# Unread products planned by the scheduler, weight loads that wait for earlier ones, and key copies on another engine, in a fused attention and two-layer expert kernel

## The chip, the core and the metric

The kernel runs on one core of a Trainium2 chip. The core has a matrix engine (TensorE, PE in the rows; PEld is its weight load), a vector engine (VectorE, DVE), a scalar engine (ScalarE, ACT), a general engine (GpSimd, POOL) and a queue engine (SyncE, SP) that issues transfers to 16 DMA engines. Each engine works off its own list of instructions in order; a list waits where an instruction needs another engine's result. The metric is the device time of one execution in microseconds (us).

## The reference

Chunked attention with a few memory rows, then two feed-forward layers over 3072 tokens (4 batches of 768), width 512, inner width 2048:

```python
for c in range(nc):                      # chunks of 32 tokens
    k_full = concat(mem_k, k[c_start - 16 : c_end + 8])
    a = softmax(q_c @ k_full.T / sqrt(64))
    out[c] = a @ concat(mem_v, v[...])
h = x @ w_in;  g = h * clip(h + 3, 0, 6) / 6;  x = g @ w_out      # first layer
h = x @ w_in;  g = max(0.01 * h, h);           out = g @ w_out    # second layer
```

Inputs are float32; the weights come as 64-bit floats.

## The kernel before

Matrices are multiplied in a high and a low part (`xh` and `xl`, and the two halves of a tile `w`), three products for each. A weight tile is loaded as 128x1024 words (`decode`, `load`), decoded to 32 bits by one ACT instruction and four on DVE (tiles `wm`, `ys` or `st`), and split in two parts (`split_w`).

The attention is cut into units of 384 tokens and four heads (`unit`) and, near the beginning, half units (`half_unit`). Each goes through the same steps: load queries and keys (`load_qk`), copy the keys' windows next to each other (`windows`), load the value rows (`load_v`, `load_whole`), copy the memory rows into them (`memory`, on POOL), scores on PE, maximum on DVE, exponential on ACT, sum and normalisation on DVE (`norm`), transposes on PE, their copy to SBUF by ACT (`take_p`), value products on PE, and `to_x`, which makes `xh` on ACT and `xl` on DVE. Four of these pieces make the first 512 tokens: two units whose PSUM tiles are `at` and `ab`, and two half units in `h` and `ac`. The products of the first layer (`hidden`, line 1003; `output`, line 1052) begin with these 512 tokens. All later attention lies between such products.

Only keys and a few load places (LOADS, WEIGHTS) are written by hand. Each step is a `Task` with a cost per engine, a key and what it comes after; `schedule` plays the engines through with those costs, picks for each free engine the ready task of the lowest key, and emits its instruction. The order in which instructions stand on each engine follows from that, and changes wherever a cost or constant changes. `feed` models the stream of PE's instructions: so many are held (HELD), and blocks of 256 come after a while (FETCH).

PE also computes products that nobody reads: `warm` multiplies `ident` by itself into the second half of the tile `ac`. They are tasks that come after named steps (`marks`); before `ac`'s scores they are 512 columns wide, behind them 256, and there they go into the tile that holds those scores (`home`). A product of float32 operands appears as two matmuls in the trace.

## Time and profile before

| what | value |
|---|---|
| median of 3 runs (1046.39 to 1047.87) | 1046.4 us |
| the profiled execution | 1049.14 us |
| its span in the profile | 1047.4 us |
| PE busy | 1035.1 us (99%) |
| DVE busy | 875.3 us (84%) |
| ACT busy | 693.7 us (66%) |
| POOL busy | 20.8 us (2%) |
| moved by DMA | 220.49 MB, 211 GB/s |

The span goes from the first to the last instruction of the profiled execution; the execution's own time has a little more around it. The rows below give starts in us from the span's start. In a row of the order of time, what stands in brackets is how long the engine was idle before it and what ended that. "Granted clock" is PE's: 1.00 is 2.4 GHz, 0.50 is 1.2 GHz.

### The profile page before, as it was taken

To read this page: it belongs to the slowest core of one execution; us is meant where nothing else is said; L and a number is where in the kernel's file an instruction comes from. 1 tells how busy PE (TensorE), PEld (TensorE's weight loads), DVE (VectorE), ACT (ScalarE), POOL (GpSimd) and SP (SyncE) were. 2 spreads that over 40 slices of the span, in tenths; PEclk is the share of its full clock that TensorE was granted. 3 is DMA by queue.
4 is the path that set the end of the run, shared out by engine and by line. 5 is a ranking of instruction groups with operands and counts; after the bars stand their busy time and mean duration, and the time that the engine had idled before them with its cause. 6 is when DMAs were issued, how large, how long until landed. Compare 5 with 4: busy or idle time off the path is not lost.

```text
span 1047.4 us, 20225 instructions
## 1 busy us (share of the span) xinstructions
PE 1035.1 (99%) x7476; PEld 850.3 (81%) x7476; DVE 875.3 (84%) x1485; ACT 693.7 (66%) x1480; POOL 20.8 (2%) x30
## 2 busy tenths in 40 slices
PE   7999999999999999999999999999999999999998
PEld 4778988888788888888888888888888888888886
DVE  6898988778998778799999899999576998566775
ACT  4786876655888555476686576785565874666753
POOL 3010000000000000000000000000000000000000
PEclk8899999999999999999999999999999999999999
DMA  9889787876887979673648778546342454423451
GB/s 265 283 216 331 241 291 230 258 229 221 262 282 239 332 225 290 239 239 123 214 144 268 253 251 280 183 158 221 111 171 81 174 193 156 173 109 96 146 181 61
DMA packets 127314, 220.49 MB, mean 211 GB/s; under 512 B 12528, under 2 KB 76016, under 8 KB 127216
## 3 DMA queue, kind: packets, MB, share of 16 engines
q1 hardware_dynamic: 127216, 219.20, 63.9%
q8 instruction: 59, 0.97, 0.4%
q14 instruction: 39, 0.32, 0.1%
HBM read 156.24 MB, written 62.91 MB: 209 GB/s over the span
## 4 chain that ended last, share of the span: by engine, by line
PE 89%; DVE 4%; DMA 3%; ACT 3%; issue 1%; SPq 0%; DVEq 0%; ACTq 0%
PE y L1327 15%; PE y L1052 13%; PE y L1495 12%; PE h L1327 10%; PE h L1495 8%; PE hx L1495 8%; PE h L1003 7%; PE hx L1327 7%; PE h L1052 2%; PE at L639 2%; DMA w<-in_raw 2%; PE at L549 1%; DVE w L345 1%; PE at L607 1%; PE ac L466 1%
## 5 line engine op out<-in xcount | busy, mean ns | idle before, releaser
L345 DVE TENSOR_TENSOR w<-w 128x512 fp32r<-128x512 f32 (+2 forms) x393 | 322.9, 854 | 25.8 <-ACT w L342 23.9
L342 ACT CAST w<-w 128x512 fp32r<-128x512 f32 (+1 forms) x290 | 223.3, 803 | 13.4 <-PE hx L1495 3.6
L1052 PE MATMUL y<-g,w 128*128 128x512 f32 (+1 forms) x540 | 125.2, 375 | 0.9 <-ACT g L342 0.7
L1327 PE MATMUL y<-w 128*128 128x512 f32 x516 | 124.6, 390 | 0.0
L1327 PEld LDWEIGHTS y<-w 128*128 128x128 f32 x516 | 96.6, 188 | 20.1
L1052 PEld LDWEIGHTS y<-g,w 128*128 128x128 f32 x540 | 94.1, 189 | 19.0 <-ACT g L342 1.2
L342 ACT CAST g<-w 128x512 fp32r<-128x512 f32 x80 | 49.4, 620 | 63.8 <-PE y L1495 23.0
L1495 PE MATMUL y<-w 128*128 128x512 f32 x384 | 90.3, 389 | 0.0
L1495 PEld LDWEIGHTS y<-w 128*128 128x128 f32 x384 | 72.1, 188 | 14.9
L1301 ACT ACTIVATE w<-w 128x512 f32<-128x512 f32 x72 | 45.0, 630 | 40.4 <-DVE w L1372 18.1
L1003 PE MATMUL h<-xh,w 128*128 128x512 f32 (+1 forms) x288 | 66.1, 370 | 0.5 <-DVE w L345 0.5
L345 DVE TENSOR_TENSOR g<-w,g 128x512 fp32r<-128x512 f32 x80 | 54.1, 684 | 14.3 <-ACT g L342 14.2
L1495 PE MATMUL h<-w 128*128 128x512 f32 x264 | 62.1, 389 | 0.0
L1495 PE MATMUL hx<-w 128*128 128x512 f32 x252 | 59.2, 389 | 0.0
L1327 PE MATMUL h<-xl,w 128*128 128x512 f32 x240 | 58.3, 391 | 0.0
L1495 PEld LDWEIGHTS h<-w 128*128 128x128 f32 x264 | 49.6, 188 | 10.3
L1003 PEld LDWEIGHTS h<-xh,w 128*128 128x128 f32 x288 | 49.7, 189 | 9.9 <-DVE w L345 0.9
L1495 PEld LDWEIGHTS hx<-w 128*128 128x128 f32 x252 | 47.3, 188 | 9.8
L1327 PEld LDWEIGHTS h<-xl,w 128*128 128x128 f32 x240 | 44.8, 188 | 9.9 <-DVE xl L345 0.4
L1327 PE MATMUL y<-xh,w 128*128 128x512 f32 x216 | 52.2, 390 | 0.0
L1327 PEld LDWEIGHTS y<-xh,w 128*128 128x128 f32 x216 | 40.5, 188 | 8.4
L1052 PE MATMUL y<-w 128*128 128x512 f32 x180 | 46.6, 391 | 0.0
(244 smaller groups left out, 1852.2 us busy)
## 6 DMA issues: line engine op xcount, KB each, us to landing
w<-kept2i SPq DMA_DIRECT2D x42, 512.0 KB
w<-kept2o SPq DMA_DIRECT2D x42, 512.0 KB
w<-kept1i SPq DMA_DIRECT2D x28, 512.0 KB
a<-in_raw SPq DMA_DIRECT2D x20, 448.0 KB
w<-in_w1i SPq DMA_DIRECT2D x16, 512.0 KB
w<-in_w1o SPq DMA_DIRECT2D x16, 512.0 KB
w<-in_w2i SPq DMA_DIRECT2D x16, 512.0 KB
w<-in_w2o SPq DMA_DIRECT2D x16, 512.0 KB
```

What stands on the lines that cost most here:

```text
L342: nc.scalar.copy(out, in_) if e == "ACT" else engine(e).tensor_copy(out=out, in_=in_)
L345: engine(e).tensor_tensor(out=out, in0=a, in1=b, op=ALU.subtract)
L466: nc.tensor.matmul(x, ident, ident.unsqueeze(1).to_broadcast([128, c, 128]), start=True, stop=True, skip_group_check=True)
L549: nc.tensor.matmul(ps.t[h * CHUNK:(h + 1) * CHUNK, par, i * W:(i + 1) * W], qk[h // 2].t[r, gp, (h % 2) * G + c * CHUNK:(h % 2) * G + (c + ...
L607: nc.tensor.transpose(pt.t[:, i // NC, (i % NC) * 128:(i % NC + 1) * 128], pview()[:, i * 128:(i + 1) * 128], ident)
L639: nc.tensor.matmul(pv.t[(h % 2) * D:(h % 2 + 1) * D, par, (h // 2) * 2 * G + i * CHUNK:(h // 2) * 2 * G + (i + 1) * CHUNK], v[h // 2].t[r, ...
L1003: nc.tensor.matmul(h.t[:, o:o + n], w.t[:, 1 if p == 1 else 0, k * 128:(k + 1) * 128], x[:, k, c0:c0 + n], start=(p == 0 and k == 0 and o ...
L1052: nc.tensor.matmul(bank(banks[d])[:, c0:c0 + n], w.t[:, 1 if p == 1 else 0, d * 128:(d + 1) * 128], g.t[:, 1 if p == 2 else 0, at:at + n], ...
L1301: return add(lambda e: nc.scalar.activation(out=at(), in_=at(), func=AF.Prelu, alpha=0.01), {"ACT": act(N)}, key, after=[after], uses=uses)
L1327: nc.tensor.matmul(bank(to), wt(l, o)[:, kt * 128:(kt + 1) * 128].bitcast(F32R), operand(p, name, 1 if q == 2 else 0, kt).bitcast(F32R), s ...
L1495: nc.tensor.matmul(bank(to[d]), wt(1 if q == 1 else 0, o)[:, d * 128:(d + 1) * 128].bitcast(F32R), g.t[:, 1 if q == 2 else 0], start=(fres ...
```

## The change

Unread products: `warm` and `marks` are gone. `schedule` gets a function `filler` and a list of places (`spots`); when PE has no task before the first product of the first layer, it emits a product of 512 columns into a place that is free (`opens` names a tile that becomes free for it at the end of a task, `closes` takes it out). It keeps a rough record of PE's work (`worked`) and doubles costs where that was low.

Weight loads: the third to sixth load get `hold`. A copy of one element on POOL (`follow`) from the weight tile two loads earlier, once that has landed, into the new tile comes ahead of the load, which thereby waits.

Copies: both copies of the keys' windows of the second unit (`ab`) go from DVE to ACT (`windows(i)`, the costs in `unit`). The memory rows (`memory`) are copied by POOL, as they were.

Constants: the costs for transfers, instruction blocks and DVE beside POOL in `schedule`.

```diff
-RATE_QK, RATE, RATE_V, COLD = 380.0, 220.0, 300.0, 1.1
+RATE_QK, RATE, RATE_V, COLD = 380.0, 220.0, 240.0, 1.1
...
-STARTS, LANDS, SURE = 1900.0, 500.0, 1500.0
-HELD, FETCHED, FETCH, STALL = 447, 256, 5000.0, 250.0
+STARTS, LANDS, SURE, SOONER = 1900.0, 250.0, (0.0, 1500.0), 20000.0
+HELD, FETCHED, ASKS, FETCH, STALL = 447, 256, (256, 356), 2500.0, 250.0
+WINDOW, PHASE, IDLE, WATCHED, BESIDE = 3413.0, 4400.0, 2000.0, 80000.0, 0.4
+FIRST, LATER, FIRST_TILL = (512, 1900.0), (512, 880.0), 2500.0
...
-            if comes is None and used >= held - FETCHED:
-                comes = at + FETCH
+            if comes is None and used >= held - ASKS[at > 45000.0]:
+                comes = max(at, max((y for x, y in queued if x <= at), default=0.0)) + FETCH if at < WATCHED else at + 2.0 * FETCH
...
                 if pick is None:
+                    if e == "PE" and not progress and spots and (begun or now < FIRST_TILL):
+                        cols, took = LATER if begun else FIRST
+                        filler(spots[0], cols)
...
+                        free[e] = end
+                        push(end, "free", None)
                     continue
...
+                    d = pick.opts[e]
+                    if now < WATCHED:
+                        at = int((now - PHASE) // WINDOW)
+                        if now < PHASE or worked.get(at - 1, 0.0) < WINDOW - IDLE:
+                            d *= 2.0
...
+                if e == "DVE" and free["POOL"] > now and pick.key < 100:
+                    d += min(BESIDE * d, free["POOL"] - now)
...
+        if hold:
+            before, landed = hold
+
+            def follow(e):
+                nc.gpsimd.tensor_copy(out=make(t, ([128, 512, 2], U32))[:1, 0, :1].bitcast(F32), in_=before.t[:1, 0, :1].bitcast(F32))
+
+            k = add(follow, {"POOL": 100.0}, early, after=[*after, landed], allocs=[t], uses=[before])
+            k = add(load, {"SP": dma(524288, 380.0)}, early, after=[k], uses=[t])
...
+    def filler(b, cols):
+        t = made(b)
+        nc.tensor.matmul((t[:, 1] if b.tag[0] == "a" else t)[:, N - cols:], ident, ident.unsqueeze(1).to_broadcast([128, cols // 128, 128]) if cols > 128 else ident[:, :cols], start=True, stop=True, skip_group_check=True)
...
-        t = [add(windows(i), ({"DVE": 850.0} if i or quad else {"ACT": 1050.0}) if j == 0 else {"ACT": 1050.0}, key - 30, after=[l1[i]], allocs=[kw[i]], uses=[qk[i]]) for i in range(2)]
+        t = [add(windows(i), ({"DVE": 850.0} if i and not quad else {"ACT": 1050.0}) if j == 0 else {"ACT": 1050.0}, key - 30, after=[l1[i]], allocs=[kw[i]], uses=[qk[i]]) for i in range(2)]
...
-    warm(2)
-    warm(1, marks["s", 0, 0])
-    warm(2, marks["s", 0, 1])
-    warm(1, marks["s", 1, 0, 0])
-    home = marks["b", 1, 1, 0][0]
-    for m, n in ((("s", 1, 1, 0), 2), (("t", 0, 0), 3), (("t", 0, 1), 3), (("t", 1, 1, 0), 2), (("v", 1, 0, 0), 2)):
-        warm(n, marks[m], home)
...
+            parts = decode(src, f, at - 8, early[i] if i < len(early) else min(at - 38, 6 * i - 40), splits[before:before + 1] if before >= 0 else (), "ys" if i % 2 else ("wm", "st")[f // 2 % 2] if alone_ else "wm", gate=behind if 3 <= i < 6 else (), own=alone_, split=which if alone_ else None, hold=arrivals[i - 2] if 2 <= i < 6 else ())
```

What that moves, at three places. PE from the unread product behind the first unit's scores on, before; `ident` as an operand means an unread product where the shape is 512 or 256 wide, and a transpose where it is 128 wide; `64x32` are value products, `32x64` scores:

```order
L466 MATMUL ac<-ident 128x512
L549 MATMUL ab<-w 32x64 x48
L466 MATMUL ac<-ident 128x512 x2
L816 MATMUL h<-w 32x64 x24
L466 MATMUL ac<-ident 128x512
L816 MATMUL ac<-w 32x64 x24
L607 MATMUL at<-ident,w 128x128 x6
L466 MATMUL ac<-ident 128x256 x5
L627 MATMUL at<-w 64x32 x48
L607 MATMUL ab<-ident,w 128x128 x6
L466 MATMUL ac<-ident 128x256 x3
```

and the same stretch after the change:

```order
L505 MATMUL ac<-ident 128x512 x2
L586 MATMUL ab<-w 32x64 x48
L505 MATMUL ac<-ident 128x512 x3
L853 MATMUL h<-w 32x64 x24
L644 MATMUL at<-ident,w 128x128 x6
L505 MATMUL ac<-ident 128x512
L853 MATMUL ac<-w 32x64 x24
L664 MATMUL at<-w 64x32 x48
L644 MATMUL ab<-ident,w 128x128 x6
L908 MATMUL h<-ident,w 128x128 x3
L505 MATMUL h<-ident 128x512
L908 MATMUL ac<-ident,w 128x128 x3
```

The transposes of `at` stand ahead of `ac`'s scores now, no unread product stands between those scores and `at`'s value products, and the two that are left before the first product go into `h`, one on each side of `ac`'s transposes.

DVE between the reciprocal of the first unit's sums and its normalisation (`TENSOR_TENSOR w<-w,mx 128x768`), before; the copies are the windows of the keys of the half unit in `ac`:

```order
L599 RECIPROCAL mx<-mx 128x12
L342 COPY w<-w 128x2x3x56
L342 COPY w<-w 128x2x3x8
L342 COPY w<-w 128x2x3x56
L342 COPY w<-w 128x2x3x8
L603 TENSOR_TENSOR w<-w,mx 128x768
```

and after:

```order
L636 RECIPROCAL mx<-mx 128x12
L640 TENSOR_TENSOR w<-w,mx 128x768
L375 COPY w<-w 128x2x3x56
L375 COPY w<-w 128x2x3x8
L375 COPY w<-w 128x2x3x56
L375 COPY w<-w 128x2x3x8
```

The normalisation now stands ahead of the copies.

SP from the last value rows of the first 512 tokens (`L783`) on, before; the pieces of 56x3x128 and 8x3x128 are value rows of the next half unit, the 128x2x448 in front of them its queries and keys, 128x1024 a weight tile:

```order
L783 DMA w<-in_raw 64x2x128 x2
L394 DMA w<-in_w1i 128x1024
L394 DMA w<-in_w1o 128x1024
L394 DMA w<-in_w1i 128x1024
L394 DMA w<-in_w1o 128x1024
L774 DMA w<-in_raw 128x2x448
L790 DMA w<-in_raw 56x3x128
```

and after:

```order
L820 DMA w<-in_raw 64x2x128 x2
L427 DMA w<-in_w1i 128x1024
L427 DMA w<-in_w1o 128x1024
L811 DMA w<-in_raw 128x2x448
L827 DMA w<-in_raw 56x3x128
```

The fifth and sixth weight load have moved behind the queries and keys of the next half unit and the eight pieces of its value rows.

## Rows read from the trace of the kernel before

**Rows 1.** Busy time by stage: stretch, its length, engines, granted clock, DMA share, GB/s.

```profile
30.00:40.00 10.00, 10.00 (x262) 8.19 (x261) 7.85 (x22) 6.57 (x21) 0.00 (x0) 0.85 0.71 208
40.00:50.00 10.00, 8.83 (x82) 6.56 (x82) 9.85 (x25) 9.92 (x33) 0.00 (x0) 1.00 0.85 308
...
400.00:500.00 100.00, 100.00 (x443) 82.83 (x442) 89.17 (x148) 62.70 (x100) 0.00 (x0) 1.00 0.65 216
```

**Rows 2.** The page's first line.

```profile
span 1047.4 us, 20225 instructions
```

**Rows 3.** PE in order of time: start, duration, line, operation, count.

```profile
1.36 3.78 PE L466 MATMUL ac<-ident 128*128 128x512 f32 x4 [1.36 <-POOL three L308]
...
8.73 1.45 PE L549 MATMUL ab<-w 64*32 64x64 f32 x96
10.11 1.99 PE L466 MATMUL ac<-ident 128*128 128x512 f32 x4
...
14.37 0.45 PE L816 MATMUL h<-w 64*32 64x64 f32 x29 [1.40 <-issue]
...
17.28 1.51 PE L607 MATMUL at<-ident,w 128*128 128x128 f32 x6
...
23.62 2.08 PE L466 MATMUL ac<-ident 128*128 128x256 f32 x4 [1.97 <-ACT w L850]
25.62 2.97 PE L627 MATMUL at<-w 64*64 64x32 f32 x96
...
39.77 2.17 PE L1003 MATMUL h<-xh,w 128*128 128x512 f32 x8
...
47.28 1.20 PE L1052 MATMUL y<-g,w 128*128 128x512 f32 x4 [0.67 <-ACT g L342]
```

**Rows 4.** Waits of PE, 40 to 1040 us: total, times, longest.

```profile
PE y L1052 <- ACT g L342: 0.7, 1, 0.7
PE at L871 <- DVE w L867: 0.5, 1, 0.5
...
PE hx L1327 <- DVE w L1294: 0.2, 1, 0.2
```

**Rows 5.** ACT in order of time, 0 to 20 us.

```profile
4.58 1.11 ACT L342 COPY w<-w 128x336 f32<-128x336 f32 x4 [2.35 <-DMA w<-in_raw]
11.10 0.84 ACT L573 ACTIVATE w<-w 128x768 f32<-128x768 f32 x1 [5.41 <-DVE w L568]
...
18.89 0.80 ACT L342 COPY w<-at 128x768 f32<-128x768 f32 x1
```

**Rows 6.** Busy time and granted clock of three stretches, columns as in rows 1.

```profile
13.00:14.40 1.40, 0.03 (x5) 0.03 (x6) 1.03 (x3) 1.40 (x11) 1.19 (x2) 1.00 1.22 324
16.00:19.50 3.50, 3.46 (x56) 2.72 (x57) 3.43 (x12) 1.32 (x4) 1.21 (x2) 0.50 1.11 312
29.60:33.00 3.40, 3.40 (x12) 2.73 (x11) 2.96 (x7) 0.88 (x2) 0.00 (x0) 0.50 0.84 231
```

**Rows 7.** The chain that ended last: later value products of a whole unit.

```profile
82.32 1.55 PE at L639 x96
```

**Rows 8.** DVE in order of time, 9 to 17 us.

```profile
9.01 0.07 DVE L563 MEMSET at<- 128x16 f32 x1
...
15.51 0.77 DVE L342 COPY w<-w 128x336 f32<-128x336 f32 x4 [1.41 <-DMA w<-in_raw]
16.19 0.95 DVE L603 TENSOR_TENSOR w<-w,mx 128x768 f32<-128x768 f32 x1
```

**Rows 9.** DMA queues, 19 to 20 us: PE's instruction blocks (packets, MB, share).

```profile
q8 instruction: 1, 0.02, 6.9%
```

**Rows 10.** POOL in order of time: memory rows of the second unit and of `ac`.

```profile
20.06 2.17 POOL L342 COPY w<-w 8x768 f32<-8x768 f32 x2 [1.78 <-DMA w<-in_raw]
...
24.69 1.55 POOL L342 COPY w<-w 8x768 f32<-8x768 f32 x2 [0.41 <-DMA w<-in_raw]
```

**Rows 11.** SP in order of time: issue of the fifth weight load.

```profile
23.54 0.43 SPq L394 DMA_DIRECT2D w<-in_w1i  x1
```

More of the change, by code (lines that the diff above doesn't have):

```diff
@@ L101, with schedule @@
 MARGIN = 300.0
-def schedule(tasks, places, ends):
+def schedule(tasks, places, ends, filler, spots):
     free = {"PE": 0.0, "DVE": 0.0, "ACT": 0.0, "POOL": 0.0, "SP": 0.0}
@@ L171, in finish @@
             if not t.left:
-                push(now + (MARGIN if "PE" in t.opts and not t.moe else 0.0), "ready", t)
+                push(now + (MARGIN if "PE" in t.opts and not t.moe and now > SOONER else 0.0), "ready", t)
     for t in tasks:
@@ L387, in tile_attn_moe_moe2, with decode @@
     wbuf, wtask = {}, {}
-    def decode(src, f, key, early=None, after=(), place="wm", gate=(), late=0, own=True, split=None):
+    def decode(src, f, key, early=None, after=(), place="wm", gate=(), late=0, own=True, split=None, hold=()):
         t, m = Buf("w"), Buf(place)
         def load(e):
-            nc.sync.dma_start(out=make(t, ([128, 512, 2], U32)).rearrange("p w s -> p (w s)"), in_=src[f])
+            nc.sync.dma_start(out=made_as(t, [128, 512, 2], U32).rearrange("p w s -> p (w s)"), in_=src[f])
         def absolute(e):
@@ L446, in tile_attn_moe_moe2 @@
     xbuf, xdone, turn, sent = {}, {}, [], {}
+    arrivals = []
     def x_buf(layer, j):
@@ L965, in half_unit @@
         t = add(norm, {"DVE": 500.0}, key - 11, after=[t], uses=[e, s])
-        t = marks["t", j, quad, gp] = add(transpose, {"PE": cold * 300.0}, key - 7, ins=6, after=[t], uses=[e, *banks])
-        t = add(take_p, {"ACT": act(NC * 128)}, key - 5, after=[t], uses=[*banks, e])
-        t = marks["v", j, quad, gp] = add(values_whole if whole else values, {"PE": cold * 900.0}, key, ins=96, after=[t, l2], uses=[e, v, *banks])
+        t = add(transpose, {"PE": cold * 300.0}, key - 7, ins=6, after=[t], uses=[e, *banks], closes=banks[:1])
+        t = add(take_p, {"ACT": act(NC * 128)}, key - 5, after=[t], uses=[*banks, e], opens=banks[0])
+        t = add(values_whole if whole else values, {"PE": cold * 900.0}, key, ins=96, after=[t, l2], uses=[e, v, *banks], closes=banks)
         jb, at = divmod(begins, N)
@@ L1412, in seven, with made_as @@
                 put(r, add(lambda e: nc.scalar.activation(out=make(r), in_=bank(ba), func=AF.Prelu, alpha=0.01), {"ACT": act(N, 50.0)}, key, after=[k, done[7]], allocs=[r], uses=[ba]))
-    def made_as(b, shape):
-        return b.t if b.t is not None else make(b, (shape, F32))
+    def made_as(b, shape, kind=F32):
+        return b.t if b.t is not None else make(b, (shape, kind))
     def waiting_parts(j, f):
@@ L1639, in tile_attn_moe_moe2 @@
         constants()
-        schedule(tasks, places, ends)
+        schedule(tasks, places, ends, filler, [begun_at])
 def kernel(**inputs):
```

67 lines of the change are left out of this document (39 added, 28 removed).

## The prediction

> **What bounds the kernel now.** I read the table by stage first [rows 1]. From 400 us on TensorE (PE) is busy the whole time: 100.00 us of 100, at the granted clock 1.00. Nothing in the change takes a product out of that part, so it keeps its length. (The two levels of that clock are 2.4 GHz, shown as 1.00, and 1.2 GHz, shown as 0.50.) What is not product work is the beginning: the span is 1047.4 us [rows 2], and the order of time on PE shows the first product of the first expert layer (`h<-xh,w`) at 39.77 us and the first output product (`y`) at 47.28 us [rows 3]. Of those 39.77 us the attention of the first 512 tokens, on all engines, is the bound, so I read the beginning engine by engine. The waits of PE between 40 and 1040 us are 2.5 us in all, six rows from 0.7 down to 0.2; the dearest, 0.7 us, stands right before that first `y` [rows 3, 4]. A microsecond won before 39.77 us therefore ends up in the total, unless something between 40 and 80 us can't follow: DVE is busy 9.85 and ACT 9.92 of 10 us in 40 to 50 us [rows 1].
>
> The beginning itself: PE does the transposes of the first unit (`at`) at 17.28 us, and ACT has copied them out at 19.69 (18.89 + 0.80, [rows 5]). The value products that need only this copy and the value rows stand at 25.62 us. In between PE is held by unread products: the group of 23.62 us waited 1.97 us for ACT, which was still reading the tile `ac` that they overwrite [rows 3]. So some 6 us of the 39.77 are a wait that the fillers themselves put into PE's queue. A second loss is the clock: 1.00 until PE had 0.03 us of work in 13.00 to 14.40, 0.50 in 16.00 to 19.50 and still in 29.60 to 33.00 us [rows 6], so that the value products took 2.97 us where the same shape takes 1.55 us at full clock [rows 7].
>
> **The change, step by step.** All times after are estimates, walked forward from the rows.
>
> Keys of the second unit by ACT. DVE loses two groups of four copies, 0.77 us each (the shape of the 15.51 row, [rows 8]); it can start on the maximum of `at` right after its scores, near 7.95 instead of 9.01. ACT takes them at 1.11 us each while it has nothing else to do: it was idle for 5.41 us before its work of 11.10 us [rows 5], so they cost nothing there. `ab`'s scores come later, though: two fillers (four passes, 1.99 us by the 10.11 row) stand ahead of them, so 9.7 instead of 8.73 [rows 3]. ACT's twelve exponentials start about 0.2 us later.
>
> DVE's normalisation of `at` now stands ahead of the copy that waited for a DMA until 15.51 us [rows 8], so it runs at 14.4 instead of 16.19, and the transposes can follow near 15.4 instead of 17.28: 1.9 us won. The scores of `h` are not won: PE stood 1.40 us without an issue until 14.37 [rows 3], in the middle of them, after some 440 instructions; the count of instructions ahead of that point is nearly the same after the change, and the added fillers fill the same gap.
>
> Fillers. 18 calls become 10, and of the ones behind `ac`'s scores two remain, in `h`. No filler waits for ACT any more; `at`'s value products follow the copy: 16.9 (transposes) + 0.9 (copy) and one filler and `ac`'s scores beside it give about 18 to 20 us instead of 25.62. Here the instruction stream comes in: the next block of instructions passes the DMA in 19 to 20 us [rows 9], and it is needed some 40% into these value products. After the block that arrived before, PE went on at 14.37; so I let PE stand to about 21 us, up to 2.4 us if it comes at full clock, nothing if it comes at half clock. The Trainium skill, "Runtime: NRT & Kernel Launch", Instruction fetch mechanics, says that crossing from one block to the next is mostly hidden; the 1.40 us row disagrees at this place, and by the page this stop would be 0 instead of up to 2.4 us. By the page alone the time would be that of rival (b).
>
> From there on the chain is PE itself, at half clock: rest of the values to 22.5 us, transposes of `ab`, `h` and `ac` (1.51 us for six [rows 3]) with two fillers of 1.9 us (3.78 for two calls) to 28.4, the three value groups (2.97, and half of it twice, with gaps) to 34.7, the last scores to 35.9 us. The other engines are ready by then: POOL's last memory rows end at 26.24 (24.69 + 1.55, [rows 10]) and don't depend on PE; ACT and DVE come to the last part of the tokens' tile (`xh`, `xl`) near 32 to 35 us. So the first product starts at 35.9 instead of 39.77: -3.9 us. It starts at half clock; in the rows PE was busy 3.40 of 3.40 us in the stretch ahead of the rise [rows 6], so I take 4 us of products at half speed: +2.0. ACT and DVE are then ahead of PE, so the waits of 0.7 and 0.5 us before the first `y` [rows 4] go: -1.2. Sum -3.1, and -0.3 for the small waits later: **-3.4 us**.
>
> Third to sixth weight load held back. The first two holds cost nothing: those loads stand behind the value rows in SP's queue as before, and the weights whose landing they wait for were issued well ahead of these. The fifth load was issued at 23.54 [rows 11] and now stands behind the keys and eight pieces of value rows, at some 29.5 us by my walk; landed at 33 us it is needed by products that stand behind the first `y` (7.5 us after the first product, [rows 3]), so not before 43. Between 0 and -0.5 us for the earlier keys, +1 if ACT must wait for it; I take 0. Behind the waiting SP stand the next keys and the seventh load. The two tiny copies on POOL stand ahead of memory rows that come later anyway (20.06, 24.69 [rows 10]).
>
> Planner's constants after 20 us. PE's order differs in about a dozen attention pieces that move by two to eight products and is the same from the middle on. With 2.5 us of waits in all in 40 to 1040, I bound it by -1 and +1.5 us and take 0.
>
> The profiled execution took 1049.14 us (span 1047.4 and 1.7 around it), the median of the three runs is 1046.4. 1049.14 - 3.4 = 1045.7 for such an execution, and on the median **1043.0 us**. Bounds of this case: clock lost half a microsecond earlier or later in the attention and the constants together, 1041.3 to 1045.0.
>
> **Rivals.** (a) *The clock comes back early.* It rose in the rows behind a stretch that held fillers [rows 6], and the two between the transposes make another one, 3.8 us of them with 0.8 between. Then the last three value groups run at full clock: 1.55 [rows 7] and two halves of about 1 instead of some 6.3 in all, products start near 33 at full clock: -6.5, and ACT and DVE give 0.5 back: 1040.4. For: these fillers are wide; against: two are few, with narrow work around them.
> (b) *The instruction block is in time* and the clock never falls: start near 31, -8: 1038.4. Only the rule of the Runtime page speaks for it, the 1.40 us row against.
> (c) *The gain is given back.* DVE at 9.85 and ACT at 9.92 of 10 us [rows 1] can't run 3 to 8 us ahead; new waits in front of `y` and the second layer's weights eat all but 0.7 us: 1045.7. For: these shares; against: DVE was idle for 2.15 of 10 us in 30 to 40 us [rows 1], where its earlier work goes, and it has two copies less.
> (d) *Slower.* PE stays at half clock well into the products, since it starts them earlier than their operands: each microsecond costs 0.5. The win of 3.9 + 1.2 is used up at 10 us of such products; at 15 us it is +2.4: 1048.8. Against: in the rows PE was at 1.00 all through 40 to 50 us though it was busy for only 8.83 of them [rows 1].
> That the change does nothing isn't one: the fillers' wait on ACT has left the order.
>
> **How the numbers follow.** Forecast (products from about 36 us, cold at first) 0.43; (a) 0.26; (b) 0.06; (c) 0.13; (d) 0.12. The prediction is 1043.0 us. Measurements of this kernel tell about 0.2% (2.1 us) from no change, so faster is below 1044.3 and slower above 1048.5. Faster: 0.36 of the forecast, (a) and (b): 0.68. Same: 0.07 of the forecast and (c): 0.20. Slower: (d), 0.12. The range leaves out (b), (d) and a few ends: 1039.5 to 1046.8.
>
> **What would show it.** Right: no wait of a filler on ACT; `at`'s values before 21 us; the clock at 0.50 in some stretch between 16 and 36; first product at 35 to 37 us; from 400 us on the same 100 of 100. (a) shows as 1.00 from about 29 us on and a first product near 33, (c) as waits of `y` or `h` for ACT or DVE of several us in 35 to 80, (d) as 0.50 in the stretch behind the first product. Wrong would be a first product after 38 us, or PE waits of over 4 us after 80 us.

## The result, and the profile after

The changed kernel takes 1053.19 us (median of 6 runs, 1052.17 to 1055.57), the kernel before in the same runs 1047.13 us: a ratio of 1.0054, 95% interval 1.0039 to 1.0068. It is slower by some 6 us. The prediction was 1043.0 us, with 1039.5 to 1046.8 as its range. The profiled execution took 1054.32 us, its span is 1052.5 us.

Busy time by stage, after (columns as in [rows 1]):

```profile
30.00:40.00 10.00, 8.67 (x195) 7.00 (x191) 8.08 (x26) 7.94 (x34) 0.00 (x0) 0.83 0.81 247
40.00:50.00 10.00, 10.00 (x134) 7.83 (x134) 9.61 (x20) 8.55 (x24) 0.00 (x0) 1.00 0.82 294
50.00:60.00 10.00, 8.50 (x75) 6.63 (x74) 9.45 (x21) 8.40 (x25) 0.00 (x0) 0.83 0.81 217
100.00:120.00 20.00, 16.81 (x289) 16.04 (x288) 16.77 (x36) 13.78 (x49) 1.64 (x1) 0.83 0.73 255
400.00:500.00 100.00, 100.00 (x443) 82.81 (x442) 87.54 (x148) 60.58 (x97) 0.00 (x0) 1.00 0.65 218
```

The two stages that differ most, in the kernel before:

```profile
50.00:60.00 10.00, 10.00 (x91) 7.97 (x91) 9.71 (x24) 7.95 (x29) 0.00 (x0) 1.00 1.03 240
100.00:120.00 20.00, 19.89 (x397) 18.95 (x397) 18.05 (x37) 17.28 (x55) 1.48 (x1) 1.00 0.86 302
```

From 400 us on nothing has changed. What is new are two stages in which PE is not full and runs at a lower granted clock: 50 to 60 us, and 100 to 120 us. PE in order of time, after (to hold against [rows 3]; L664 are value products of a whole unit, L1039 is `hidden`, L1088 `output`, L908 the transposes of a half unit):

```profile
17.32 0.88 PE L664 MATMUL at<-w 64*64 64x32 f32 x37
21.25 1.88 PE L664 MATMUL at<-w 64*64 64x32 f32 x59 [3.04 <-issue]
...
33.90 0.73 PE L1039 MATMUL h<-xh,w 128*128 128x512 f32 x2
...
42.18 2.09 PE L1088 MATMUL y<-g,w 128*128 128x512 f32 x8
...
53.23 0.52 PE L908 MATMUL at<-ident,w 128*128 128x128 f32 x3 [0.65 <-DVE w L904]
54.59 1.13 PE L936 MATMUL at<-w 64*64 64x32 f32 x48 [0.84 <-ACT w L375]
55.66 3.65 PE L1039 MATMUL h<-xh,w 128*128 128x512 f32 x8
...
107.95 1.65 PE L1039 MATMUL h<-xh,w 128*128 128x256 f32 x6 [3.19 <-ACT xh L375]
```

The start came out as hoped, even better: the first product at 33.90 us (39.77 in [rows 3]), the first `y` at 42.18 (47.28). Then it is lost. I counted the product instructions of the expert layers in order of time and held the start of the n-th after against the n-th before, at counts ahead of which both kernels have done the same attention work: -5.9 us at the first, -5.2 at the 60th (52 us after), -1.7 at the 84th (63 us), -2.5 at the 144th (79 us), +3.2 at the 288th (114 us), +4.8 at the 480th (157 us), and +5.6 at the last. The first loss is the half-clock stretch behind two waits of 0.65 and 0.84 us (eight products in 3.65 us, which take 1.98 at full clock). The second, 5.7 us, is for the most part the wait at 107.95 us and the half clock behind it. Busy time and clock there (columns as above):

```profile
105.00:108.00 3.00, 0.05 (x1) 0.05 (x1) 0.33 (x1) 1.29 (x5) 0.00 (x0) 0.80 0.57 218
108.00:111.00 3.00, 3.00 (x102) 2.69 (x102) 2.73 (x7) 1.39 (x4) 0.00 (x0) 0.50 0.44 89
```

ACT in order of time says what PE waited for: the cast of `xh` stands behind the decoding of a weight into `ys`, and that waits for the buffer that a store of `half` still reads.

```profile
102.26 1.31 ACT L375 CAST w<-wm 128x512 fp32r<-128x512 f32 x2
106.71 0.66 ACT L430 ACTIVATE ys<-w 128x512 f32<-128x512 f32 x1 [3.14 <-DMA half<-ys]
107.27 0.63 ACT L375 CAST xh<-at 128x384 fp32r<-128x384 f32 x2
```

The chain of waits has that store as one piece, 10.21 us from its issue to its landing:

```profile
96.42 10.21 DMA half<-ys
```

In the kernel before the same cast stands ahead of that weight:

```profile
101.87 0.65 ACT L342 CAST xh<-at 128x384 fp32r<-128x384 f32 x2 [1.13 <-PE at L639]
...
105.91 0.71 ACT L397 ACTIVATE ys<-w 128x512 f32<-128x512 f32 x1
```

The waits of PE in 36 to 1060 us, the first rows (to hold against [rows 4]):

```profile
PE h L1039 <- ACT xh L375: 3.2, 1, 3.2
PE at L586 <- issue: 1.4, 3, 0.6
PE at L644 <- ACT w L375: 0.9, 1, 0.9
PE at L936 <- ACT w L375: 0.8, 1, 0.8
PE at L908 <- DVE w L904: 0.7, 1, 0.7
```

So two questions: is it the planner's new order that costs, and would the gain of the start have arrived without it?

### The profile page after: what moved, and what is told of

Same layout as the page of the kernel before. It is cut to its first block, busy times and chain, and to the rows that moved or that the text cites. A ratio compares the mean times of both kernels' runs of the same rounds, so it can differ in the third digit from the quotient of the medians.

```text
span 1052.5 us, 20185 instructions
## 1 busy us (share of the span) xinstructions
PE 1033.5 (98%) x7460; PEld 849.4 (81%) x7460; DVE 877.2 (83%) x1479; ACT 697.6 (66%) x1485; POOL 23.9 (2%) x35
## 4 chain that ended last, share of the span: by engine, by line
PE 91%; DMA 4%; ACT 2%; DVE 2%; issue 1%; SPq 0%; ACTq 0%
PE y L1363 16%; PE y L1088 13%; PE y L1531 12%; PE h L1363 11%; PE h L1531 8%; PE hx L1363 8%; PE hx L1531 8%; PE h L1039 6%; PE h L1088 2%; DMA w<-in_raw 2%; PE at L676 2%; PE at L586 1%; DMA half<-ys 1%; DMA a<-in_raw 1%; PE at L644 1%
## 5 line engine op out<-in xcount | busy, mean ns | idle before, releaser
L1088 PE MATMUL y<-g,w 128*128 128x512 f32 (+1 forms) x540 | 124.7, 374 | 0.8 <-DVE g L378 0.5
L1363 PE MATMUL y<-w 128*128 128x512 f32 x516 | 124.1, 390 | 0.0
L1088 PEld LDWEIGHTS y<-g,w 128*128 128x128 f32 x540 | 94.4, 188 | 18.8 <-ACT w L375 0.8
L375 ACT CAST g<-w 128x512 fp32r<-128x512 f32 x80 | 49.7, 624 | 65.3 <-PE y L1531 22.5
L1531 PE MATMUL y<-w 128*128 128x512 f32 x384 | 90.3, 389 | 0.0
L1039 PE MATMUL h<-xh,w 128*128 128x512 f32 (+1 forms) x288 | 71.2, 388 | 3.8 <-ACT xh L375 3.8
L1039 PEld LDWEIGHTS h<-xh,w 128*128 128x128 f32 x288 | 52.7, 202 | 14.1 <-ACT xh L375 4.4
L1531 PEld LDWEIGHTS hx<-w 128*128 128x128 f32 x252 | 47.3, 188 | 9.8
L1408 DVE TENSOR_TENSOR w<-y,w 128x512 f32<-128x512 f32 x35 | 24.0, 690 | 30.6 <-PE y L1363 27.9
```

The source lines that it names most:

```text
L375: nc.scalar.copy(out, in_) if e == "ACT" else engine(e).tensor_copy(out=out, in_=in_)
L1039: nc.tensor.matmul(h.t[:, o:o + n], w.t[:, 1 if p == 1 else 0, k * 128:(k + 1) * 128], x[:, k, c0:c0 + n], start=(p == 0 and k == 0 and o ...
L1088: nc.tensor.matmul(bank(banks[d])[:, c0:c0 + n], w.t[:, 1 if p == 1 else 0, d * 128:(d + 1) * 128], g.t[:, 1 if p == 2 else 0, at:at + n], ...
L1363: nc.tensor.matmul(bank(to), wt(l, o)[:, kt * 128:(kt + 1) * 128].bitcast(F32R), operand(p, name, 1 if q == 2 else 0, kt).bitcast(F32R), s ...
L1408: done[2] = add(lambda e: nc.vector.tensor_tensor(out=half_of(x, 0), in0=bank(bb), in1=ut.t[:, 0], op=ALU.add), low, key, after=[k, done[1 ...
L1531: nc.tensor.matmul(bank(to[d]), wt(1 if q == 1 else 0, o)[:, d * 128:(d + 1) * 128].bitcast(F32R), g.t[:, 1 if q == 2 else 0], start=(fres ...
```

## The experiments

**One place, and the parts of the change.** Theory T1: the start's 5 us are real and the new order loses them, at a few places. T2: engines and transfers can't carry an earlier start, whatever the order. T3: the held weight loads are to blame. The first run removes the costliest place alone, the `ys` weight ahead of `xh`:

```diff
-gate=behind if 3 <= i < 6 else ()
+gate=behind if 3 <= i < 6 else [t for t, c in xdone['1', 1][0] if t.key < 60] if at - 8 == 121 else ()
```

> The changed kernel with one edge more: the absolute value of the weight of key 121, which needs the `ys` buffer that a store of `half` frees, may stand on ACT only behind the `xh` part of the unit of key 54. Up to that point all instructions stand as in the changed kernel. T1 (the start is really 5 us earlier and the planner's later order loses it at single places): the wait of TensorE for `xh` near 108 us (3.2 us) and the half-clock stretch behind it (about 3.5 us) go, 7 us in all, and little comes back: 1046 to 1048 us. T2 (whatever the order, ACT, DVE and the transfers can't carry an earlier start through 40 to 115 us): the wait shows up again within 10 us, at a weight or at `y`, and the time stays at 1051 to 1053 us.

1050.86 us, ratio 1.0029 (1.0018 to 1.0039), between what T1 and T2 had named. The place itself is mended: at the 288th product it stands at -2.2 us instead of +3.2. But of these 5.3 us only 2.3 are in the time, by the medians. The order behind it came out differently again (+1.5 us at the 516th product, +4.6 at the last), and new waits appear, the first rows of PE's waits in this run:

```profile
PE at L586 <- ACT a L375: 1.2, 3, 0.8
PE h L1363 <- ACT xl L375: 1.2, 1, 1.2
PE y L1088 <- ACT g L375: 1.0, 1, 1.0
```

Next, the planner's constants of the kernel before from the first product on (`progress` is zero until then; `RATE_V` keeps its new value):

```diff
-if comes is None and used >= held - ASKS[at > 45000.0]:
+if comes is None and used >= held - (FETCHED if progress else ASKS[at > 45000.0]):
-    comes = max(at, ...) + FETCH if at < WATCHED else at + 2.0 * FETCH
+    comes = at + 5000.0 if progress else max(at, ...) + FETCH if at < WATCHED else at + 2.0 * FETCH
-lanes[e].append(wire + LANDS)
+lanes[e].append(wire + (500.0 if progress else LANDS))
...
-if now < WATCHED:
+if now < WATCHED and not progress:
```

> The changed kernel with the planner's constants of the kernel before from the first product of the first layer on (transfers land 500 ns after the wire instead of 250, instruction blocks asked for at 256 and due after 5 us, no slower DVE beside POOL, no doubled cost). The attention of the first 512 tokens, its fillers, copies and held loads stand as in the changed kernel. T1: first product at 33.9 us as in the changed kernel, no wait above 1 us between 100 and 115 us, 1042 to 1047 us. T2: 1050 to 1054 us, with the loss between 50 and 115 us again, perhaps at another place.

1054.11 us, 1.0063 (1.0050 to 1.0076). No better: the order is again another one. It has the first product at 32.79 us and is 1.7 us ahead at the 336th, and loses 6.6 us by the 360th. The costliest wait there, from PE in order of time, is for `g`:

```profile
117.70 0.73 PE L1088 MATMUL y<-g,w 128*128 128x256 f32 x4 [2.40 <-ACT g L375]
```

So it is not the constants that were put back, as such. The holds and the copies alone:

```diff
-own=alone_, split=which if alone_ else None, hold=arrivals[i - 2] if 2 <= i < 6 else ())
+own=alone_, split=which if alone_ else None)
```

> The changed kernel without the holds: the third to sixth weight load are issued as soon as SP comes to them. T3 (the holds make weights late behind the start and are the cause of the loss): the waits of ACT for `w` near 47.8 and 57.8 us go, the clock stays at 1.00 in 50 to 60 us, under 1049 us. T1: the start is 0 to 2 us later than 33.9 us since value rows share the wire with weights; the order behind it is another one, in which `xh` stands ahead of that `ys` weight, so the 104 to 114 us loss goes as well: 1046 to 1050 us, and 50 to 60 us lose about as much as before. T2: 1052 us or more.

1053.46 us, 1.0058 (1.0042 to 1.0073). And the kernel before with nothing but the copies moved:

```diff
-({"DVE": 850.0} if i or quad else {"ACT": 1050.0})
+({"DVE": 850.0} if i and not quad else {"ACT": 1050.0})
```

> The kernel before with one edit: both key copies of the second unit on ACT instead of DVE. By my prediction's walk the transposes of `at` come 1 to 2 us earlier, but the value products still stand behind the filler that waits for ACT to leave `ac`, so the first product stays within 1 us of 39.8 us and the time within 2 us of the kernel before: 1045 to 1048 us. If the copies alone carry the earlier start, the first product is below 37 us.

1051.34 us, 1.0037 (1.0022 to 1.0052). I had expected at most 2 us either way. The first product is at 36.75 us, which I had named as the sign that the copies alone carry the earlier start; but the kernel before has it anywhere from 35.3 to 39.8 us (below), so this sign tells nothing. A change of cost and engine for one step, at 4 to 9 us of 1047, gives another order from there on, with 2.5 us of waits of `y` for `g`. T3 is out as the single cause; T1 and T2 are still mixed up, since every edit draws a new order.

**Start and order taken apart.** So I took the order out of the planner's hands. The order in which it emits the kernel before's 4999 common steps, with their engines, was written down as a list; in the changed kernel `schedule` stops at its first product and emits what is left by that list.

```diff
     while events:
+        if progress:
+            break
...
+    while turn_of:
+        for i, (t, e) in enumerate(turn_of):
+            if not t.left and blocked(t) is None:
+                break
+        turn_of.pop(i)
...
+        t.fn(e)
```

> The changed kernel up to the planner's first product of the first layer (fillers, copies, held loads and all that is issued ahead of it), and behind that every remaining step in the order, and on the engine, that it has in the kernel before. Order is the only thing that differs from the changed kernel, and it has nothing of its planner's later choices. T1 (the later order loses the gain): first product at 33.9 us, 5 us ahead of the kernel before at the first `y`, and of these 3 to 5 us stay: 1042 to 1045 us. T2 (engines and transfers can't carry an earlier start): the 5 us shrink to under 1.5 us by 115 us: 1046 to 1049 us. Waits of TensorE at single places up to 1.5 us are expected by both.

1048.32 us, 0.9997 (0.9986 to 1.0007): the same as the kernel before. The reverse, the kernel before up to its first product and the changed kernel's order behind it:

> The reverse: the kernel before up to its first product of the first layer, and behind that every step in the changed kernel's order. T1: the losses of that order (4 us in 50 to 60 us, 7 us in 104 to 114 us, some 3 us behind) are added to a start without gain: 1055 to 1061 us. T2: with TensorE 6 us later the operands are there in time and most of the losses vanish: 1048 to 1052 us.

1053.16 us, 1.0044 (1.0026 to 1.0061), between what T1 and T2 had named. The costly place of the changed kernel is there with the old start too: ACT waits for the same store, and PE for the cast behind it:

```profile
104.37 0.66 ACT L603 ACTIVATE ys<-w 128x512 f32<-128x512 f32 x1 [1.55 <-DMA half<-ys]
```

```profile
105.62 0.97 PE L1209 MATMUL h<-xh,w 128*128 128x256 f32 x6 [1.60 <-ACT xh L548]
```

Against the kernel before this run stands at -2.7 us at the 144th product, +0.3 at the 288th, +0.9 at the 336th and +2.4 at the last: 3.6 of these 5.0 us arise in 78 to 118 us. The four corners:

| | old order | new order |
|---|---|---|
| old start | 1 | 1.0044 |
| new start | 0.9997 | 1.0054 |

The order costs 4.6 us behind the old start and 6.0 behind the new one (0.0044 and 0.0057 of 1047); the start is worth nothing measurable. T1 holds for the order and T2 for the start. Two more runs put the point of return later, `progress >= 36` and `progress >= 84` in place of `progress`:

> The changed kernel up to its 36th step of products (about 78 us), the order of the kernel before for all that is left. T1: the loss at 53 to 59 us is in, those behind 100 us are not: 1044.5 to 1047.5 us. T2: as the run whose order goes back at the first product, within 1 us.

1047.26 us, 0.9991 (0.9980 to 1.0002), in T1's range, and not to be told from the run that goes back at the first product.

> The changed kernel up to its 84th step of products (about 118 us), the order of the kernel before for all that is left. T1: both early losses are in (3.5 us behind the kernel before at that point), the one of 128 to 205 us is not: 1050 to 1052.5 us. If the loss behind 120 us has nothing to do with the order, it stays at 1053 to 1055 us.

1055.08 us, 1.0065 (1.0052 to 1.0078), over both numbers expected. It is 1.9 us behind at the 336th product (118.6 us), 6.0 at the 360th (128.3 us; 125.8 in the changed kernel), and nothing is added behind that. So 2.8 us arise between its 144th product (-0.9) and the point of return, and 4.1 us in the 10 us behind that point, where the two orders meet; the second part says nothing on the changed kernel's order. What the two runs show together: the new order costs nothing that lasts ahead of its 36th step (78 us), and in the changed kernel itself 5.7 us arise between the 144th and the 336th product (-2.5 to +3.2 us, 79 to 120 us). That the loss of 53 to 59 us is in the earlier of the two runs and costs nothing there (-4.7 us at the 60th product, -0.7 at the 84th, -1.5 at the 144th) fits T2: what is lost early had no worth. PE in order of time in the later of the two, 100 to 124 us, the rows with a wait: the one for `xh` again, and, behind the point of return, one for POOL's normalisation in the next unit:

```profile
107.13 0.98 PE L1245 MATMUL h<-xh,w 128*128 128x256 f32 x6 [1.30 <-ACT xh L581]
108.65 1.61 PE L792 MATMUL at<-w,a 64*32 64x64 f32 x96 [0.55 <-ACT st L636]
121.58 1.09 PE L850 MATMUL at<-ident,w 128*128 128x128 f32 x6 [2.72 <-POOL w L846]
```

**Why the old order doesn't carry the new start.** PE in order of time with the new start and the old order (the list stands in the file, so line numbers are higher: L1245 is `hidden`, L1294 `output`):

```profile
31.62 0.67 PE L1130 MATMUL ac<-w 64*64 64x32 f32 x15 [3.57 <-issue]
...
33.12 3.78 PE L1245 MATMUL h<-xh,w 128*128 128x512 f32 x8
...
41.63 0.52 PE L1114 MATMUL at<-ident,w 128*128 128x128 f32 x3 [0.99 <-ACT r L1260]
43.26 1.70 PE L1294 MATMUL y<-g,w 128*128 128x512 f32 x4 [1.11 <-ACT g L581]
...
46.35 3.78 PE L1294 MATMUL y<-g,w 128*128 128x512 f32 x8
...
122.70 2.11 PE L1245 MATMUL h<-xh,w 128*128 128x512 f32 x8
```

6.65 us ahead at the first product, 1.5 at the 36th: the first eight products run at half clock, then come two waits, then half clock again (3.78 for what takes 2.11). The last row is the one at 123.64 us in the kernel before: 0.9 us of the gain is left. Three candidates: the clock lost in the two waits, the first `y`s' place in the order, the held loads. First, two unread products fill the two waits:

```diff
         def transpose(eng):
+            if gp and not quad:
+                filler(banks[0], 512)
...
             def fn(e):
+                if begin and j == 0 and f == 0 and lay == "1" and some[0] == (0, 0):
+                    bank(banks[0])
+                    filler(banks[0], 512)
```

> The new start with the order of the kernel before behind it, and two unread products of 512 columns more: one ahead of the transposes at 41.6 us, where TensorE waited 1.0 us, one in the bank of the first `y`, where it waited 1.1 us. Clock theory (the win of the start is lost since TensorE is idle 2.1 us in 40.6 to 43.3 us and then runs at half clock to 50 us): the clock stays at 1.00 in 44 to 50 us, the eight output products take 2.1 us instead of 3.8, 2.5 to 3 us stay, 1044.5 to 1046.5 us. Bound theory (ACT and DVE only now have the operands ready, half clock or not): the products wait for operands instead, at least 2 us more of waits between 44 and 65 us, 1047 to 1049 us.

1047.34 us, 1.0001 (0.9991 to 1.0010). The clock stayed at 1.00 in 45 to 50 us and PE had no wait over 0.5 us in 44 to 65, so the bound theory's own sign is missing; and still the 2.3 us that it had at the 36th product are 1.5 at the 132nd, 1.6 at the 336th and 0.8 at the 516th (163 us); held against a second execution of the kernel before (below), nothing is left there. Then the changed order up to the 15th step, which has its 5 us at 52 us:

> The changed kernel up to its 15th step of products (about 52 us, where it is 5 us ahead of the kernel before and has no wait of TensorE ahead of the first `y`), the order of the kernel before behind that. Clock theory: without the waits of 41 to 43 us the clock holds, and the order of the kernel before has no late operands at 53 to 59 us: 3 us or more stay, 1044 to 1046 us. Bound theory: DVE is at its limit in 45 to 55 us, TensorE waits 1 us or more at the transposes or the next hidden products in 52 to 60 us whatever the order: 1046.5 to 1049 us.

1047.65 us, 1.0000 (0.9990 to 1.0009). -4.8 us at the 60th product, -1.1 at the 108th, 0 at the 156th (86 us). PE waits 2.2 us at 67 us for a weight, and ACT, which makes it, had waited for attention inputs. The waits of ACT in 34 to 122 us in this run (total, times, longest):

```profile
ACT w L581 <- DMA w<-in_raw: 4.2, 4, 2.4
...
ACT ys L636 <- DMA w<-in_w1o: 1.9, 4, 1.0
ACT wm L636 <- DMA w<-in_w1i: 1.9, 1, 1.9
ACT ys L636 <- DMA half<-ys: 1.7, 2, 0.9
ACT w L581 <- DMA a<-in_raw: 1.7, 2, 0.9
```

11.4 us for transfers, where the kernel before has a single row of 1.3 us. Last, the fifth and sixth load without a hold (`2 <= i < 4`):

> The new start with the order of the kernel before behind it, only the third and fourth weight load held; the fifth and sixth are issued when SP comes to them. T3 (ACT waits 2.2 and 1.1 us for the weights of the fifth and sixth load at 35 to 38 us, and this delays the first `g`): these waits go, the first `y` no longer waits, 1044.5 to 1046.5 us. Without T3: the value rows of the half units come later by what the two loads take of the wire, the first product is 0 to 2 us later, 1047 to 1049 us.

1047.80 us, 1.0003 (0.9993 to 1.0013); the first product moves to 37.67 us in this execution, further than the 0 to 2 us that I had set without T3, and again nothing changes in the time. By now the first `y` had been at 42.5, 43.3, 45.0, 47.0 and 47.3 us and the time always the same. The suspect is supply: the transfers of weights and inputs, which don't start earlier because PE does.

**The start made later, and half of the weight bytes.** If supply paces the kernel, a later start is free as well. Three unread products of 512 columns ahead of the first product of the kernel before:

```diff
                 if p == 0 and o == 0:
                     make(h)
+                    if lay == "1" and j == 0 and f == 0:
+                        for _ in range(3):
+                            nc.tensor.matmul(h.t, ident, ident.unsqueeze(1).to_broadcast([128, 4, 128]), ...)
```

> The kernel before with three unread products of 512 columns ahead of the first product of the first layer, so that TensorE begins it some 3 us later (39.8 to 42.8 us); nothing else differs. My prediction's step (a microsecond at the start is a microsecond in total): +3 us, 1050 to 1051 us. Supply theory (what comes behind the start is paced by the transfers of weights and attention inputs and by ACT and DVE behind them, not by TensorE's start): the 3 us shrink in 45 to 115 us to under 1.5 us: 1047.5 to 1049 us.

1048.87 us, 1.0003 (0.9992 to 1.0013): they take 2.28 us on PE (36.79 to 39.07 us) and cost 0.3 us, by the interval -0.8 to 1.4:

```profile
36.79 2.84 PE L1003 MATMUL h<-ident 128*128 128x512 f32 x6
39.07 2.42 PE L1006 MATMUL h<-xh,w 128*128 128x512 f32 x8
```

Six of them:

> The kernel before with six unread products of 512 columns ahead of the first product, some 4.6 to 5.5 us of work (three took 2.3 us). Supply theory: the first cost of a late start shows once it is later than the transfers need: 0.5 to 3 us over the kernel before, less than what was added. If the start counted fully from the first microsecond, the three would have shown, and six cost 4.6 us or more.

1050.51 us, 1.0023 (1.0014 to 1.0032): 4.85 us of products (35.51 to 40.36 us) cost 2.4, as expected. In the profiled execution 1.3 us of that stand at the 361st product (123.77 us; 122.47 in the run below), and 1.6 more arise at 163 to 180 us, where ACT waits 3.0 us for a store and 1.4 us for attention inputs. And the kernel before against itself:

> The kernel before, unchanged, timed against itself. Two uses: how far a ratio lies from 1 where nothing differs (expected 0.999 to 1.001), and one more execution of its start. If the start of the first profile (39.8 us, TensorE at 1.20 GHz through 16 to 33 us) is what the kernel usually does, the first product stands at 39 to 40.5 us again; if that execution was a late one, as the same instructions in two other runs suggest (35.3 and 36.8 us), it stands at 34.5 to 37.5 us.

1.0004 (0.9994 to 1.0015), and a first product at 37.17 us, not 39.77. To relieve the transfers, each weight load of the first layer moves only the first 512 words of each row, into the first half of its tile, and the decoding reads that half twice; the other half of the weights is left out:

```diff
-in_=src[f])
+in_=src[f][:, :512])
...
+        def twice(word):
+            return t.t[:, :256, word].unsqueeze(1).to_broadcast([128, 2, 256])
```

The decoding itself takes as long as before (0.70 us for one ACT instruction, 0.68 us for one of those on DVE that read the tile, in both), so it is the transfers that the edit relieves. Under the old start, the new start with the old order, the new start with the two unread products, and the old start with three unread products ahead of the first product:

> The kernel before, in which each weight load of the first layer moves half its bytes (the first 512 of 1024 words of each row); the decoding reads that half twice, so the weights are not the reference's, and every instruction is there as before. It is the base for the next two. Supply theory: a little faster than the kernel before, 0.5 to 2.5 us, since its own start doesn't wait for weights. If transfers don't matter: within 0.5 us of it.

1043.06 us, 0.9957 (0.9940 to 0.9974): 4.5 us by the ratio, 5.5 by the medians, more than the 2.5 named.

> The new start with the order of the kernel before behind it, with the half weight loads of the run before this (same part of the weights left out). Supply theory: ACT's waits for weights in 34 to 84 us (5.3 us with whole loads) fall under 2 us, and of the 5 to 6 us of the start at least 2.5 us more than with whole loads stay against the same kernel with the old start: 2.5 to 5 us under the run before this. If ACT and DVE themselves are the limit, transfers aside: within 1 us of the run before this.

1041.87 us, 0.9935 (0.9921 to 0.9950).

> As the last, with the two unread products at the first `y` as well. Supply theory: the clock is kept and the operands are there: 3 to 6 us under the kernel before with half loads. If ACT and DVE are the limit: within 1 us of it.

1043.44 us, 0.9951 (0.9936 to 0.9966).

> The kernel before with half weight loads (the second half of each row of the first layer's weights left out, as in the earlier run of that kind) and three unread products of 2.3 us ahead of the first product. Supply theory: with the transfers relieved TensorE's own start sets the pace, and the same 2.3 us that cost nothing with whole loads cost 1.5 to 2.5 us: 1044.5 to 1045.6 us against 1043.06. If something else than transfers swallows a late start, it costs under 0.7 us here too.

1047.25 us, 0.9989 (0.9975 to 1.0004): with half the bytes the same 2.28 us of unread products that had cost nothing measurable cost 4.2 us by the medians (3.4 by the ratios, some 1 to 6 by their intervals), more than they take and more than I had expected. The mean granted clock of each execution tells the two shares apart. At 0.998 or more lie six of the eight executions without the three products (1042.3 to 1043.6 us) and four of the nine with them (1044.4 to 1045.6 us); their medians differ by 1.9 us (2.5 when each is held against the kernel before timed beside it), for 2.28 us of products. The others have 0.992 to 0.997 and take 1046.3 to 1050.4 us. So with half the bytes the products cost what they take, and clock that is lost is paid for too. With whole loads the kernel before took on average 1047.7 us in 44 executions at 0.998 or more and 1047.9 us in 66 at 0.994 to 0.997 (1049.8 us in 14 below that); where they lost it no trace shows. PE in order of time in the first and the last of the four, first `y` and the row that stands at 123.64 us in the kernel before:

```profile
41.89 1.20 PE L1058 MATMUL y<-g,w 128*128 128x512 f32 x4 [0.68 <-ACT g L342]
...
117.95 2.11 PE L1009 MATMUL h<-xh,w 128*128 128x512 f32 x8
```

```profile
49.56 1.23 PE L1061 MATMUL y<-g,w 128*128 128x512 f32 x4 [0.95 <-ACT g L342]
...
125.73 2.11 PE L1012 MATMUL h<-xh,w 128*128 128x512 f32 x8
```

7.7 us later at the first `y` (2.28 of it the unread products; the rest is a start at half clock, whose first unread product stands at 39.96 us), and 7.8 us later at the other row. All runs in which the old order stands between these two rows (in the two that go back at steps 15 and 36, only behind 52 and 78 us), by the start of the first `y`; ACT's waits for transfers are the sum of its rows in 34 to 122 us:

| run | first `y` | the later row | between | ACT's waits for transfers |
|---|---|---|---|---|
| new start, order back at 15 | 42.49 | 124.86 | 82.4 | 11.4 |
| new start, order back at 36 | 42.54 | 122.63 | 80.1 | 6.0 |
| new start | 43.26 | 122.70 | 79.4 | 5.6 |
| old start, before again | 44.65 | 122.47 | 77.8 | 4.7 |
| new start, two unread products | 45.02 | 122.71 | 77.7 | 8.4 |
| old start, three unread products | 46.41 | 123.08 | 76.7 | none |
| new start, two holds | 47.05 | 123.38 | 76.3 | 1.0 |
| old start, before | 47.28 | 123.64 | 76.4 | 1.3 |
| old start, six unread products | 47.68 | 123.77 | 76.1 | none |
| half bytes, old start | 41.89 | 117.95 | 76.1 | none |
| half bytes, new start | 42.02 | 118.17 | 76.2 | 1.7 |
| half bytes, new start, two unread products | 43.54 | 120.06 | 76.5 | none |
| half bytes, old start, three unread products | 49.56 | 125.73 | 76.2 | none |

This settles where a gain at the start goes. The later row is the 361st product in every run, and the work between the two rows takes 76 us when nothing is late. With half the weight bytes it takes 76.1 to 76.5 us from wherever it starts, 41.89 or 49.56 us. With whole loads it takes as little only when the first `y` stands at 46 to 47 us or later; an earlier one only stretches it, and ACT then stands waiting for transfers. The kernel before sat just at that knee. The waits do not add up to the stretch one for one (8.4 us of them go with 1.3 us), and which transfers decide, those of weights or those of attention inputs behind them, stays open.

My numbers for the runs with half bytes were wrong in one more way: I expected the new start to beat the old one there by 2.5 to 5 us, and it does so by 1.2, with intervals that overlap; with the two unread products, 3 to 6 us expected, it is 0.4 us behind. With less traffic the old start had its first `y` at 41.89 us, as early as the new one.

No version beats the kernel before: the best with whole loads, 0.9991 (0.9980 to 1.0002), can't be told from it.

## Why the prediction was wrong, point by point

*The start.* Right in its mechanism: no filler waits for ACT, `at`'s value products begin at 17.32 us (18 to 20 forecast, 25.62 before), the first product moved by 5.9 us between the two profiles (3.9 forecast). The stop of the instruction block behind those products took 3.04 us (up to 2.4 forecast). The clock went as rival (a) said: 0.50 in 21.5 to 28.0 us, 1.00 from 28.5 on, first product at 33.90 (33 there), and half clock once more for most of the first eight products:

```profile
21.50:28.00 6.50, 6.50 (x71) 5.00 (x67) 6.08 (x13) 3.37 (x9) 3.74 (x5) 0.50 0.85 266
28.50:33.50 5.00, 4.23 (x226) 3.74 (x227) 3.52 (x13) 3.05 (x14) 0.18 (x1) 1.00 0.67 163
```

That was this execution: with the same start and the old order behind it the clock was 1.00 in 21.5 to 28.0 us, and the first product stood at 33.12 all the same. One sum of the walk is short: by its own terms (1.51 twice and 3.78 us from 22.5 us on) the transposes and the two fillers end at 29.3 us, not 28.4; they took 5.7 us (23.05 to 28.79), so the slip decided nothing.

*The base.* The gain was counted from one execution whose start was late. Five executions of the old start, whole loads, had their first product (or the first unread one put ahead of it) at 35.26, 35.51, 36.79, 37.17 and 39.77 us; the profile of before was the 39.77. Eight of the new start stand between 32.79 and 34.67. Between the middle ones lie 3 us, not 5.9. I saw that the execution was 2.7 us over the median and took these off the result, without asking whether they sat in the very stretch from which I took the gain.

*The step that failed.* "A microsecond won before 39.77 us therefore ends up in the total, unless something between 40 and 80 us can't follow." The transfers can't: 6.65 us won at the first product left 0.3 us of 1047 (0.9997, 0.9986 to 1.0007), and with whole loads the stretch behind the first `y` grows as the start comes earlier. I had judged what could follow by the waits of PE, 2.5 us in all [rows 4], and by busy shares of DVE and ACT [rows 1]. But PE's waits show what was late for the old start, not what would be late for an earlier one. Rival (c) had the shape of it and the wrong limit: it named DVE and ACT, and was given 0.13; the runs with half bytes show the transfers. Its 1045.7 us counted 0.7 us of gain as left; measured is 0.3, and nothing by the interval.

*The term that was mis-sized.* On the planner's constants after 20 us: "I bound it by -1 and +1.5 us and take 0." Measured +4.6 us behind the old start, +6.0 behind the new one. My ground was that the order differed in a dozen pieces only and that the waits were 2.5 us in all. The second is a property of one order: four other orders that the same planner drew (the first four runs) cost 1.0029 to 1.0063. The prediction's own sign for "wrong", waits of PE of over 4 us after 80 us, is there (3.2, 1.4 and 0.9 us in the rows for `h` and for L586 and L644, all behind 80 us).

*Rival (d).* Products at half clock behind an early start did occur (0.83 in 30 to 40 us, and the 3.65 us row), but they are part of a loss that was free, not the cause of the 6 us. The half clock that counts is the one at 108 us, behind a wait that the new order makes.

*The holds at 0.* Right in the time by the run with two holds; ACT did wait for the weights that came late (2.2 us for one, with the new start and the old order), but that too was free. *The copies at no cost on ACT.* Right as work, but moving them redraws the order: 1.0037 by themselves.

What stays open: the cost of the new order is placed, not taken apart. Behind either start most of it arises in 78 to 120 us, with the wait for `xh` behind the `ys` weight in it: 5.7 us behind the new start, 3.6 behind the old. Mending that one place gave 2.3 of the 6 us in the time, since another order came behind it. What arises behind 120 us (2.4 and 1.5 us) I have not taken apart.

## What to carry to other kernels

Before costing a gain at the head of a pipeline, make the head later by a known length: if 2.3 us of dummy products cost nothing, the head does not set the time, and a gain there is worth nothing either; the run that shows it takes one edit. Where a planner draws the order, an edit of any cost is also a new order; hold the order fixed as a list to see what the edit itself is worth, and hold several orders against each other before calling one good. And read a start from several executions, since one profile may hold its late case.

## What the runs showed of the hardware that I had not expected

The same instructions at the start ran at either clock level from one execution to the next. Busy time and granted clock in 24 to 33 us, the kernel before, the run with the old start and the new order, and the kernel before again:

```profile
24.00:33.00 9.00, 9.00 (x115) 7.44 (x115) 5.78 (x13) 2.45 (x7) 1.77 (x3) 0.50 0.93 321
```

```profile
24.00:33.00 9.00, 8.79 (x236) 7.42 (x230) 8.46 (x23) 5.95 (x19) 1.81 (x3) 1.00 0.95 309
```

```profile
24.00:33.00 9.00, 9.00 (x177) 7.93 (x172) 5.89 (x13) 4.25 (x10) 1.71 (x3) 0.63 0.86 302
```

PE had stood 1.40, 0.82 and 0.72 us without an issue near 14 us in these three, and only after the first the clock was 0.50 in 16 to 20 us already.

Two stops of PE without an issue come at the same two instructions in every execution of the new start with whole loads and all holds, ahead of the last 59 value products of `at` and the last 15 of `ac`, and their lengths vary: 0.4 to 3.4 us at the first, 0.7 to 3.6 us at the second, in eight executions. I read them as the change from one instruction block to the next: in the changed kernel a packet of the instruction queue passes in 18 to 19 and in 30 to 31 us, 2 to 3 us ahead of PE's next instruction. In the two executions with a first stop under 1 us the second is over 3.2 (0.39 and 3.30 us, 0.69 and 3.57 us); in the changed kernel they are 3.04 and 0.77 us. So the first product stays at 32.8 to 34.7 us; that the next block is the limit there is read from these rows, not tried. The Trainium skill, "Runtime: NRT & Kernel Launch", Instruction fetch mechanics, calls the crossing mostly hidden; here one of the two was the longest wait of PE between its first work and the first product in each of the eight.

The first of four stores of `half` (128 x 512 floats each, by their tile) took 10.21 us from its issue to its landing, with seven loads and stores issued in the 4 us ahead of it; a buffer that such a store holds is not free when its data has been read by everyone else (ACT waited 3.14 us for this one).
